# A fused attention and MLP kernel: quads 0 and 1 scored in three rounds of 512 columns with a shared 64-row key tile, and a new order of the first table

## Chip, cores and metric

The kernel runs on one core of a Trainium2 chip. The metric is the device time of one execution in microseconds. Engines: PE is TensorE (matmuls), PEld its weight loads, DVE is VectorE, ACT is ScalarE, POOL is GpSimd, SP is SyncE. POOL issues most of the loads of the first part, and ACT does the exponentials and gelus.

## What is computed

The reference is a causal attention with a forget gate, then an MLP with a tanh gelu. Cut to what matters:

```python
# q, k, v: (8, 8, 576, 64), f: (8, 8, 576); w_in: (512, 2048), w_out: (2048, 512)
scores = scale * np.matmul(q, k.transpose(0, 1, 3, 2))
cum = np.cumsum(np.log(np.clip(f, 0.0001, 1.0)), axis=-1)
scores = np.where(causal, -1e9, scores + cum[:, :, :, None] - cum[:, :, None, :])
attn = softmax(scores)
x = np.matmul(attn, v).transpose(0, 2, 1, 3).reshape(4608, 512)
h = x @ w_in
out = gelu_tanh(h) @ w_out
```

## The kernel before, in words

**Quads.** The 64 heads are taken four at a time; quad i holds heads 4(i % 2) to 4(i % 2) + 3 of batch i // 2. Two quads fill one batch's rows of xT, the input of the MLP. The MLP goes in nine chunks of 512 rows of x; chunk 0 needs all of quads 0 and 1 except the last 64 queries.

**Scores.** The scores are computed with keys on the partitions and queries along the columns, so the key tile is the stationary operand. kT has 64 zero columns ahead of the keys and 64 behind. Causality removes all queries ahead of a key tile, so only pieces (key tile, column in pt, first query, number of queries) are computed. For quads from 2 on, `pieces` (L51) packs them in 1536 columns: the tiles "low" (64 zero rows, then keys 0 to 63) and "high" (keys 512 to 575, then 64 zero rows) share the columns 0 to 63, since each has zeros where the other has keys. The 1536 columns are done in three rounds of 512. For quads 0 and 1, `split_pieces` (L61) holds them in four rounds of 384, 512, 320 and 384 columns, 1600 in all; "high" has columns of its own there, and no "low" is used. Queries 0 to 255 (part 0) and 256 to 575 (part 1) are finished separately, so that the first half of chunk 0 can begin early.

**One round** (`scores`, L267): two passes c over the two halves of the head dimension (32 rows each), one matmul for each piece and head into PSUM (two heads in a tile of two banks, pool psS of two tiles, which the J tiles use too), then an exponential by ACT into pt for each pair of heads (L293). Word S does four heads side by side, word H one pair g of heads. After that come the causal masks: word M by affine select on POOL (L299), word m by a product on DVE (L329).

**Products** (`product`, L333): the denominators (word D: stationary w_bf, then two transposes and a reciprocal on DVE, L374 to L378) and the two halves of the head dimension (word V: stationary vw, then a product on DVE into xT, L387). With a part they use one bank of pool psM (two banks, L341), without one psO or psS (L355). vw is v times the weight of its key (word vw on DVE, VW on POOL, L233). Where "low" is used, word CL or cl copies the first 64 rows of vw to the low tile (L238), and w_bf needs the same copy (`cast_w`, L777; word w on ACT for quads 0 and 1, W on DVE for the others).

**The order.** The kernel has no loop order of its own: all engines follow tables of words (L71 to L111), written out by hand, each issuing its instructions in the order of the words. Inside an engine the order is strict; across engines semaphores order. FRONT covers quads 0 to 6 and chunks 0 and 1; SECOND, STEADY, FLUSH and LAST the rest. The words of FRONT that matter here:

- `B.n.w`: n idle matmuls of w columns (L258); `BK.i.n`: n idle matmuls of 512 columns that read kT of quad i and so wait for its transpose (L264).
- `SC`, `CT`, `CE.n`: running sum of log f on DVE, its transposes on PE (L749), the weights by exponentials on ACT (L754), n = 1 those of quads 2 on.
- `TK.i`, `TQ.i`: transposes of k and q on DVE (L216). `LK.i`, `LQ.i`: their loads (L209).
- `LP.t`: v tile t of batch 0 (tile 4 has only 64 rows); `LC.b.t` of batch b; `WI.c`: quarter c // 2 of w_in's columns, half c % 2 of its rows (L198); `WO.c`: quarter c of w_out's rows (L202). All are issued by POOL, in the order of the words, among its masks. A load waits until the eighth load before it has landed.
- `J.half.g`, `j.half.g.n`: 256 rows of chunk 0 times quarter g of w_in, 16 units of one matmul each (L439); a quarter needs WI.2g for its rows 0 to 255 and WI.2g+1 for the others. j has its PSUM tile in psO (one buffer) and goes n units on; J uses psS. `RJ` copies a finished tile out of psO, `GJ` is the gelu of a j tile, J has its own.
- `F.c.n`, `f.c.n`: n units of the second matmul of chunk c; f in tiles of 32 columns, the form of D and V. In chunk 0 a unit is one matmul of 512 columns, in the order of w_out's quarters, eight units for each in the first pair of row blocks (L692).
- `I`, `U`, `G`, `UW`, `PW`, `X`: the first matmul of chunk 1 and the sums for the Strassen products, and a preload of the exponential table.

PE changes its tile form between words: 128 x 128 for B, BK, J and F, 32 x 128 for S and H, 128 x 32 for D, V and f.

Of the kernel before, what the change touches and what calls it, by code (L numbers as in the profile page):

```python
# [16 lines left out]
def kernel(  # L17
# [53 lines left out]
    FRONT = """  # L71
        B.1.128 B.1.512 B.1.256 SC B.8.512 B.1.256 B.1.512 B.1.128 LP.0 LP.1 CT B.2.512 WI.1 B.1.256 TK.0 B.1.128 B.1.128 BK.0.2 WI.0 LP.4
        BK.0.1 B.1.512 CE.0 TQ.0 B.1.512 CE.1 LP.3 B.1.512 BK.0.1 S.0.0 B.1.128 B.1.128 LP.2 TK.1 M.0.0 w.0 WI.5 BK.0.1 B.3.512 WI.2 H.0.2.1
        WI.3 B.1.128 TQ.1 BK.0.1 B.1.128 B.1.128 B.1.256 B.1.128 BK.1.1 B.1.512 H.0.1.0 WI.4 D.0.0 vw.0.0 vw.1.0 H.0.2.0 B.2.512 BK.1.1
        B.1.128 H.1.0.1 H.1.0.0 M.1.0 B.1.128 B.1.512 B.1.128 B.1.512 B.1.128 V.0.1.0 H.1.2.0 H.0.1.1 V.0.0.0 H.0.3.0 D.1.0 V.1.1.0 j.0.0.4
        M.0.1 UT LQ.2 WI.7 V.1.0.0 H.0.3.1 H.1.3.1 j.0.0.4 j.0.0.8 H.1.1.0 vw.0.1 WI.6 H.1.1.1 RJ.0.0 M.0.3 D.0.1 LK.2 WO.1 WO.0 j.0.1.8
        VW.1.1 H.1.2.1 tr H.1.3.0 M.1.3 V.0.1.1 V.0.0.1 J.0.2 j.0.1.8 M.1.1 D.1.1 V.1.0.1 V.1.1.1 GJ.0.1 W.1 TQ.2 J.0.3 J.1.1 GJ.0.0 J.1.3
        J.1.0 U.0 WO.2 J.1.2 LK.3 WO.3 LQ.3 LC.1.0 PW.2.1 PW.2.2 F.0.3 LC.1.3 f.0.2 LC.1.4 LC.1.1 LC.1.2 TK.2 f.0.1 LK.4 LQ.4 f.0.1 S.2.0
        F.0.5 TK.3 m.2.0 F.0.5 S.2.2 F.0.2 f.0.5 TQ.3 f.0.2 S.2.1 f.0.3 LV.2.1 F.0.6 S.3.0 F.0.2 m.2.1 vw.2 cl.2 F.0.2 f.0.1 LV.2.0 X M.2.2
        D.2 M.3.0 LQ.5 f.0.1 S.3.1 VW.3 f.0.2 V.2.0 LK.5 TQ.4 TK.4 f.0.4 S.3.2 LV.3.1 LQ.6 f.0.1 m.3.1 f.0.3 LK.6 V.2.1 M.3.2 f.0.3 S.4.1  # L80
        f.0.1 F.0.5 VW.4 TQ.5 F.0.1 X H.4.2.0 H.4.2.1 D.3 f.0.1 cl.3 H.4.0.0 H.4.0.1 V.3.1 v.3.0 vw.5 U.1 f.0.2 m.4.2.2 I.1.2 I.1.1 UW.2.4
        TK.6 I.1.0 CL.5 U.2 m.4.2.3 I.1.3 I.1.5 TQ.6 U.3 TK.5 I.1.4 G.0 I.1.6 M.4.1 I.1.7 F.1.1 G.1.1.2 cl.4 F.1.5 LV.3.0 F.1.5 S.5.0 F.1.5
        M.5.0 F.1.7 m.4.0 F.1.2 UW.2.3 F.1.2 LK.8 F.1.7 LK.7 D.4 S.5.1 F.1.17 LQ.8 F.1.1 S.5.2 M.5.2.3 M.5.2.2 f.1.2 V.4.0 f.1.1 M.5.1 f.1.8
        LQ.7@m.3.1 f.1.1 V.4.1 S.6.0 M.6.0 f.1.4 D.5 f.1.10 S.6.1 f.1.1 M.6.1 f.1.2 V.5.1 vw.6 F.1.4 CL.6 F.1.5 S.6.2 m.6.2.3 V.5.0 f.1.4
        m.6.2.2 f.1.3
    """
# [174 lines left out]
    def keep_busy_after(i, n):  # L261

        for _ in range(n):
            nc.tensor.matmul(idle_ps[0][:, 0:512], idle[:, 0:128], kT[i % 2][:, 64:64 + 256, :].rearrange("p s c -> p (s c)"),  # L264
                             start=True, stop=True)

    def scores(i, r, groups=((0, 1, 2, 3),)):  # L267

        qq, p = qT[i % 2], pt[i % 2]
        if i < 2:  # L270
            off, n = split_rounds[r]
            todo = [(key, col - off, q0, nq) for (key, col, q0, nq) in split_pieces[r]]
        else:
            off, n = rounds[r]
            todo = []
            for (key, col, q0, nq) in pieces:
                a, z = max(col, off), min(col + nq, off + n)
                if a < z:
                    todo.append((key, a - off, q0 + a - col, z - a))
        for heads in groups:  # L280
            tiles = {g: psS.tile([128, 2, 512], FP32, name="ps_s", tag="s") for g in sorted({h // 2 for h in heads})}
            for c in range(2):
                for j, (key, c0, q0, nq) in enumerate(todo):
                    for h in heads:
                        nc.tensor.matmul(  # L285
                            tiles[h // 2][:, h % 2, c0:c0 + nq],
                            key_columns(i, key, h, c),
                            qq[32 * h:32 * h + 32, q0:q0 + nq, c],
                            start=(c == 0 and j == 0), stop=(c == 1),
                            skip_group_check=True,  # L290
                        )
            for g, t in tiles.items():
                nc.scalar.activation(p[:, 2 * g:2 * g + 2, off:off + n], t[:, :, 0:n], AF.Exp, scale=scale)  # L293

    def mask(i, r, keys=None):
        p = pt[i % 2]

# [4 lines left out]

        if i < 2:
            for (key, col, n) in diagonals(r, keys):
                keep(p[:, :, col:col + n], [[0, 4], [1, n]])
            return
# [11 lines left out]

    def mask_by_product(i, r, keys=None):
        p = pt[i % 2]  # L320
        if i < 2:
            todo = [(0, col, n) for (key, col, n) in diagonals(r, keys)]
        else:
            todo = [(1 if key == "low" else 0, col, 128) for (key, col, q0, nq) in pieces
                    if (not keys or key in keys) and q0 == 128 * (0 if key == "low" else 9 if key == "high" else key)
                    and rounds[r][0] <= col < rounds[r][0] + 512 and key != 0]
# [4 lines left out]
        return did

    def product(i, groups, spare, part=None):  # L333
        p = pt[i % 2]
        if part is not None:
            s0, s1 = parts[part]
            po = psM.tile([128, 512], FP32, name="po_m", tag="m")
            for (key, col, q0, nq) in sorted(sum(split_pieces[1:] if part else split_pieces[:1], []), key=lambda x: HIGH if x[0] == "high" else x[0]):
                for (r0, lhsT, h) in groups:
                    w = lhsT(HIGH if key == "high" else key)  # L340
                    nc.tensor.matmul(  # L341
                        po[r0:r0 + w.shape[-1], q0 - s0:q0 - s0 + nq], w, p[:, h, col:col + nq],
                        start=(key == 0), stop=(key == (HIGH if part else 1)),
                        skip_group_check=True,
                    )
# [431 lines left out]
    def cast_w(copy, n):  # L777
        i0, i1 = (0, 2) if n == 0 else (2, NQ)
        copy(w_bf[:, i0:i1, 0:NT, :], wT[:, i0:i1])
        if n:  # L780
            copy(w_bf[64:128, :, LOW, :], wT[0:64, :, 0, :])
# [114 lines left out]
```

## Time and profile before

| what | value |
|---|---|
| median of 3 runs | 321.03 us (321.01 to 321.31) |
| the profiled execution, in all | 321.58 us |
| its span, first to last instruction | 319.9 us |
| busy PE / DVE / ACT / POOL | 314.1 / 243.3 / 213.0 / 108.2 us |
| HBM read / written | 36.85 / 9.44 MB |
| PE clock granted | 1.00 |

A line of the timeline has start, duration, engine, line, operation, written and read tiles, tile form, shape and count; adjacent instructions of one line are merged. A line of the busy times by stretches has the stretch, its length, busy time of each engine with the number of instructions, the granted clock, the mean busy share of the 16 DMA engines (over 1 where transfers overlap) and GB/s. A line of the DMA issues has destination and source, queue, count, size and microseconds from issue to landing. Line numbers are those of the kernel before.

### The profile page before, as it was taken

The numbers are of one execution on the slowest core, as the hardware profiler recorded it, in microseconds if no ns is written. First come the engines' busy times: TensorE is split into PE (matmuls) and PEld (weight loads), VectorE is DVE, ScalarE is ACT, GpSimd is POOL, SyncE is SP. The second block draws the span as 40 slices with busy tenths as digits, with TensorE's granted clock in tenths as the row PEclk, the third lists the DMA queues.
The fourth block names the chain that finished last, engine by engine and source line by source line (L and its number), as shares of the span: only waits on it lengthen the run. The fifth ranks groups of instructions, "written<-read, shape, count | busy, mean of one in ns | idle before, by whom it ended". The sixth has DMA issues, their size and how long they took to land.

```text
span 319.9 us, 11741 instructions
## 1 busy us (share of the span) xinstructions
PE 314.1 (98%) x5292; PEld 220.7 (69%) x5311; DVE 243.3 (76%) x368; ACT 213.0 (67%) x248; POOL 108.2 (34%) x146
## 2 busy tenths in 40 slices
PE   8999999999999999999999999999999999999996
PEld 3467834445776567776778877767776786688785
DVE  7675638698978879879877998599886866597674
ACT  3676777866766776878667867787596744836610
POOL 8789625600340416400851065305610150000000
PEclk9999999999999999999999999999999999999999
DMA  7999998951273911594129411971002111010213
GB/s 125 229 199 196 207 234 202 220 150 37 54 130 103 200 22 37 115 209 77 37 75 223 104 39 30 209 160 38 5 33 68 35 33 38 24 43 2 98 35 99
DMA packets 47491, 33.41 MB, mean 104 GB/s; under 512 B 29777, under 2 KB 42193, under 8 KB 47441
## 3 DMA queue, kind: packets, MB, share of 16 engines
q0 software_dynamic: 9632, 15.99, 28.3%
q1 hardware_dynamic: 37664, 16.60, 19.4%
q8 instruction: 41, 0.67, 0.9%
q10 hardware_dynamic: 144, 0.07, 0.1%
q14 instruction: 10, 0.07, 0.1%
HBM read 36.85 MB, written 9.44 MB: 145 GB/s over the span
## 4 chain that ended last, share of the span: by engine, by line
PE 98%; DVE 1%; issue 1%
PE ps_w L619 31%; PE ps_h L403 19%; PE ps_s L285 10%; PE ps_q L539 10%; PE po L355 9%; PE ps_h L439 5%; PE pso L692 4%; PE ps_u L487 4%; PE idle_ps L258 3%; PE po_m L341 2%; PE ps_p L619 1%; PE ps_o L355 0%; PE idle_ps L264 0%; DVE xT L387 0%; PE cum_ps L749 0%
## 5 line engine op out<-in xcount | busy, mean ns | idle before, releaser
L293 ACT ACTIVATE pt<-ps_s 128x1024 bf16<-128x1024 f32 (+2 forms) x100 | 94.0, 991 | 37.5 <-PE ps_s L285 35.9
L299 POOL TENSOR_SCALAR_AFFINE_SELECT pt<-pt 128x512 bf16<-128x512 bf16 (+3 forms) x70 | 43.3, 629 | 108.3 <-ACT pt L293 85.6
L403 PE MATMUL ps_h<-xT,w_in_sb 128*128 128x512 bf16 (+1 forms) x307 | 65.5, 357 | 0.8 <-issue 0.2
L403 PEld LDWEIGHTS <-w_in_sb 128*128 128x128 bf16 x320 | 31.1, 98 | 26.5 <-issue 0.6
L411 ACT ACTIVATE gT<-ps_h 128x1024 bf16<-128x1024 f32 x34 | 34.6, 1018 | 20.3 <-PE ps_h L403 20.1
L619 PEld LDWEIGHTS <-gT 128*32 128x32 bf16 (+1 forms) x1177 | 43.9, 97 | 5.7 <-issue 2.2
L619 PE MATMUL ps_w<-w_out_sb,gT 128*32 128x256 bf16 (+1 forms) x996 | 42.7, 273 | 0.0
L619 PEld LDWEIGHTS <-gsum 128*32 128x32 bf16 (+1 forms) x909 | 35.1, 97 | 3.9 <-issue 1.7
L285 PE MATMUL ps_s<-qT,kT 32*128 32x64 bf16 (+5 forms) x896 | 35.2, 261 | 0.0
L555 DVE TENSOR_TENSOR usnap<-ps_q,usnap 128x1024 f32<-128x1024 f32 x15 | 17.9, 1221 | 17.3 <-PE ps_q L539 12.7
L619 PE MATMUL ps_w<-usum,gsum 128*32 128x256 bf16 (+1 forms) x752 | 29.8, 273 | 0.0
L233 POOL TENSOR_TENSOR vw<-v_nat,wT 128x1280 bf16<-128x1280 f32 (+1 forms) x12 | 27.4, 2279 | 2.7 <-DMA v_nat<-in_v_dram 2.4
L285 PEld LDWEIGHTS <-kT 32*128 32x128 bf16 x896 | 16.2, 92 | 16.8 <-issue 10.2
L636 DVE COPY snap<-ps_w 128x512 f32<-128x512 f32 x32 | 21.8, 682 | 6.5 <-PE ps_w L619 6.3
L550 ACT ACTIVATE gT<-usnap 128x1024 bf16<-128x1024 f32 x15 | 15.8, 1052 | 11.0 <-DVE usnap L555 10.7
L387 DVE TENSOR_TENSOR xT<-po,rb 128x576 bf16<-128x576 f32 x26 | 19.5, 751 | 4.6 <-PE po L355 4.4
L355 PE MATMUL po<-pt,vw 128*32 128x64 bf16 (+4 forms) x624 | 22.6, 278 | 0.0
L355 PEld LDWEIGHTS <-vw 128*32 128x32 bf16 x672 | 14.6, 97 | 9.6 <-issue 3.0
L216 DVE STREAM_TRANSPOSE kT<-k_c 128x576 f32<-128x576 f32 x16 | 19.4, 1244 | 2.1 <-DMA k_c<-in_k_dram 2.1
L216 DVE STREAM_TRANSPOSE qT<-q_c 128x576 f32<-128x576 f32 x16 | 19.8, 1245 | 0.3 <-DMA q_c<-in_q_dram 0.3
L209 POOL DMA_DIRECT2D k_c<-in_k_dram x16 | 9.1, 572 | 29.0 <-DVE kT L216 17.4
L539 PEld LDWEIGHTS <-w_in_sb 128*128 128x128 bf16 x160 | 15.6, 98 | 2.1
(135 smaller groups left out, 489.6 us busy)
## 6 DMA issues: line engine op xcount, KB each, us to landing
out_dram<-o_st SPq DMA_DIRECT2D x35, 256.0 KB, 2.2
k_c<-in_k_dram POOLq DMA_DIRECT2D x16, 288.0 KB, 5.5
q_c<-in_q_dram POOLq DMA_DIRECT2D x16, 288.0 KB, 6.6
v_nat<-in_v_dram SPq DMA_DIRECT2D x16, 256.0 KB, 5.3
v_nat<-in_v_dram SPq DMA_DIRECT2D x20, 128.0 KB, 5.3
v_nat<-in_v_dram POOLq DMA_DIRECT2D x8, 256.0 KB, 10.0
w_in_sb<-in_moe_w_in_dram POOLq DMA_DIRECT2D x8, 256.0 KB, 8.6
w_out_sb<-in_moe_w_out_dram POOLq DMA_DIRECT2D x4, 512.0 KB, 10.6
```

The costliest lines, as they stand in the source:

```text
L216: return nc.vector.transpose(out=dst.rearrange("p s c -> p (s c)").bitcast(FP32) .rearrange("p (t a) -> p a t", a=n), in_=src.rearrange("p ...
L233: return eng.tensor_mul(vw[i % 2][:, t0:t1], vb[:, t0:t1, h0:h0 + 4, :], wT[:, i, t0:t1, :].unsqueeze(3).to_broadcast([128, t1 - t0, 4, D]))
L285: nc.tensor.matmul(tiles[h // 2][:, h % 2, c0:c0 + nq], key_columns(i, key, h, c), qq[32 * h:32 * h + 32, q0:q0 + nq, c], start=(c == 0 an ...
L293: nc.scalar.activation(p[:, 2 * g:2 * g + 2, off:off + n], t[:, :, 0:n], AF.Exp, scale=scale)
L299: nc.gpsimd.affine_select(out=x, in_=x, compare_op=ALU.is_ge, fill=0.0, base=0, pattern=pattern, channel_multiplier=-1)
L355: nc.tensor.matmul(po[r0:r0 + w.shape[-1], 448 + q0:448 + q0 + nq], w, p[:, h, col:col + nq], start=(key in (0, "low")), stop=(key in ("lo ...
L387: nc.vector.tensor_mul(xT[:, 2 * u + x, r0 + s0:r0 + s1], po, rbs[i, part])
L403: nc.tensor.matmul(ph[:, j, n * cols:(n + 1) * cols], w_in_sb[:, dt, 128 * ft:128 * ft + 128], xT[:, dt, h0:h0 + cols], start=(dt == 0 and ...
L411: nc.scalar.activation(gelus(c, 2 * pr, 2), ph, AF.Gelu_apprx_tanh)
L539: nc.tensor.matmul(ps[:, k, HC * n:HC * n + HC], w[:, d, 128 * n:128 * n + 128], x[:, d, :], start=(first and n == 0 and d == 0), stop=(d ...
L619: nc.tensor.matmul(ps[c0:c0 + width, n, cols[0]:cols[1]], x[:, j, 128 * n + c0:128 * n + c0 + width], w[:, j, cols[0]:cols[1]], start=(fir ...
L636: copy(kept[name], ps)
```

## The change

Quads 0 and 1 get their own list of pieces in the packed 1536 columns, with "low" and "high" on the columns 0 to 63, and the three rounds of the other quads. A piece that would cross the border of the two parts (query 256) or of a round is cut there, so there are nine pieces instead of seven. Round 0 holds all of part 0 and the high tile. `scores`, `mask` and `mask_by_product` use one path for all quads, `product` picks the pieces of its part by their first query, and `cast_w` now copies the low rows in both of its calls, where the copy in W covered all quads before. CL.0 and CL.1 come in; the words of round 3 (H.0.3.x, H.1.3.x, M.x.3) go.

```diff
-    split_rounds = [(1152, 384), (0, 512), (512, 320), (832, 384)]
-    split_pieces = [
-        [(0, 1152, 0, 256), (1, 1408, 128, 128)],
-        [(0, 0, 256, 320), (3, 320, 384, 192)],
-        [(1, 512, 256, 320)],
-        [(2, 832, 256, 320), ("high", 1152, 512, 64)],
+    early_pieces = [
+        ("low", 0, 0, 64),
+        (0, 64, 64, 192),
+        (1, 256, 128, 128),
+        (1, 384, 256, 128),
+        (0, 512, 256, 320),
+        (3, 832, 384, 192),
+        (1, 1024, 384, 192),
+        (2, 1216, 256, 320),
+        ("high", 0, 512, 64),
     ]
...
+    def layout(i):
+        return early_pieces if i < 2 else pieces
...
         qq, p = qT[i % 2], pt[i % 2]
-        if i < 2:
-            off, n = split_rounds[r]
-            todo = [(key, col - off, q0, nq) for (key, col, q0, nq) in split_pieces[r]]
-        else:
-            off, n = rounds[r]
-            todo = []
-            for (key, col, q0, nq) in pieces:
+        off, n = rounds[r]
+        todo = []
+        for (key, col, q0, nq) in layout(i):
...
-            for (key, col, q0, nq) in sorted(sum(split_pieces[1:] if part else split_pieces[:1], []), key=lambda x: HIGH if x[0] == "high" else x[0]):
+            mine = [x for x in early_pieces if s0 <= x[2] < s1]
+            for (key, col, q0, nq) in sorted(mine, key=lambda x: {"low": -1, "high": HIGH}.get(x[0], x[0])):
                 for (r0, lhsT, h) in groups:
-                    w = lhsT(HIGH if key == "high" else key)
+                    w = lhsT({"low": LOW, "high": HIGH}.get(key, key))
...
         copy(w_bf[:, i0:i1, 0:NT, :], wT[:, i0:i1])
-        if n:
-            copy(w_bf[64:128, :, LOW, :], wT[0:64, :, 0, :])
+        copy(w_bf[64:128, i0:i1, LOW, :], wT[0:64, i0:i1, 0, :])
```

FRONT is new as a whole; SECOND, STEADY and the others keep their words. Up to the end of J, FRONT before reads (L72 to L78):

```
B.1.128 B.1.512 B.1.256 SC B.8.512 B.1.256 B.1.512 B.1.128 LP.0 LP.1 CT B.2.512 WI.1 B.1.256 TK.0 B.1.128 B.1.128 BK.0.2 WI.0 LP.4
BK.0.1 B.1.512 CE.0 TQ.0 B.1.512 CE.1 LP.3 B.1.512 BK.0.1 S.0.0 B.1.128 B.1.128 LP.2 TK.1 M.0.0 w.0 WI.5 BK.0.1 B.3.512 WI.2 H.0.2.1
WI.3 B.1.128 TQ.1 BK.0.1 B.1.128 B.1.128 B.1.256 B.1.128 BK.1.1 B.1.512 H.0.1.0 WI.4 D.0.0 vw.0.0 vw.1.0 H.0.2.0 B.2.512 BK.1.1
B.1.128 H.1.0.1 H.1.0.0 M.1.0 B.1.128 B.1.512 B.1.128 B.1.512 B.1.128 V.0.1.0 H.1.2.0 H.0.1.1 V.0.0.0 H.0.3.0 D.1.0 V.1.1.0 j.0.0.4
M.0.1 UT LQ.2 WI.7 V.1.0.0 H.0.3.1 H.1.3.1 j.0.0.4 j.0.0.8 H.1.1.0 vw.0.1 WI.6 H.1.1.1 RJ.0.0 M.0.3 D.0.1 LK.2 WO.1 WO.0 j.0.1.8
VW.1.1 H.1.2.1 tr H.1.3.0 M.1.3 V.0.1.1 V.0.0.1 J.0.2 j.0.1.8 M.1.1 D.1.1 V.1.0.1 V.1.1.1 GJ.0.1 W.1 TQ.2 J.0.3 J.1.1 GJ.0.0 J.1.3
J.1.0 U.0 WO.2 J.1.2 LK.3 WO.3 LQ.3 LC.1.0 PW.2.1 PW.2.2 F.0.3
```

and after the change:

```
SC LP.0 B.1.128 B.1.512 LP.3 B.8.512 B.1.512 B.1.128 B.2.512 TK.0 B.1.256 B.1.128 B.1.128 BK.0.2 LP.1 B.1.512 TQ.0 S.0.0 BK.0.1
B.1.512 B.1.128 CT CE.1 H.0.1.0 TK.1 CE.0 WI.1 w.0 B.1.128 BK.0.1 B.3.512 B.1.128 TQ.1 LP.2 WI.3 B.1.128 B.1.256 vw.0.0 WI.0 M.0.0
WI.2 LQ.2 H.1.0.0 H.1.0.1 M.1.0 LP.4 B.1.128 B.1.128 BK.0.1 BK.1.1 BK.0.1 CL.0 H.0.2.0 D.0.0 WI.4 V.0.0.0 WI.5 WI.6 WI.7 H.0.1.1
V.0.1.0 M.0.1 BK.0.1 B.1.128 B.1.128 B.1.512 B.1.128 B.1.256 vw.1.0 CL.1 H.0.2.1 H.1.2.1 UT B.1.512 LK.2 D.1.0 V.1.0.0 B.1.512
V.1.1.0 H.1.2.0 M.0.2 j.0.0.4 j.0.0.4 j.0.0.8 M.1.2 VW.1.1 H.1.1.0 H.1.1.1 WO.0 M.1.1 RJ.0.0 LC.1.1 LK.3 D.0.1 LQ.3 j.0.1.8 j.0.1.8
J.0.2 vw.0.1 GJ.0.1 V.0.0.1 TQ.2 GJ.0.0 tr PW.2.1 D.1.1 J.0.3 V.1.0.1 V.0.1.1 V.1.1.1 J.1.2 J.1.1 J.1.0 J.1.3 F.0.3 W.1 WO.1 WO.2
WO.3 LC.1.3 LC.1.2 F.0.2
```

Behind J both tables hold the same numbers of F and f units (64 for chunk 0, 97 for chunk 1), the same S, D, V and I words in a slightly different order, and a few masks, copies and sums on another engine (m.3.2 for M.3.2, M.4.2.3 for m.4.2.3, CL.3 for cl.3, cl.5 for CL.5, PW.2.4 for UW.2.4).

More of the change, by code (lines that the diff above doesn't have):

```diff
@@ L76 @@
[L76 to L79, printed above, removed]
@@ L98 @@
+        Q.0.2 Q.0.2 LB.2.3 TK.3 LB.2.4 LK.5 i.0.3.4 Q.0.2 TK.4 TQ.4 F.-1.99 I.0.6 i.0.7 G.0 S.3.0 X G.1.1.2 f.0.16 M.3.0 D.2 VW.3 f.0.12
+        S.3.1 M.3.1 V.2.0 f.0.13 S.3.2 M.3.2 CL.3 V.2.1 VW.4 f.0.15 S.4.0 D.3 f.0.10 V.3.0 M.4.0 CL.4 S.4.1 f.0.14 M.4.1 V.3.1 S.4.2 F.0.12
+        M.4.2
     """
@@ L301, in keep @@
                 fill=0.0, base=0, pattern=pattern, channel_multiplier=-1)
[L303 to L306, printed above, removed]
         if r == 0:
@@ L309, in mask @@
             keep(p[64:128, :, 0:128].rearrange("p h (b x) -> p h b x", x=64), [[0, 4], [0, 2], [1, 64]])
-        for (key, col, q0, nq) in pieces:
-            if key in (keys or (1, 2, 3)) and rounds[r][0] <= col < rounds[r][0] + 512:
+        for (key, col, q0, nq) in layout(i):
+            if key in (keys or (1, 2, 3)) and q0 == 128 * key and rounds[r][0] <= col < rounds[r][0] + 512:
                 keep(p[:, :, col:col + 128], [[0, 4], [1, 128]])
-    def diagonals(r, keys):
-        return [(4 if key == "high" else key, col, min(nq, 128)) for (key, col, q0, nq) in split_pieces[r]
-                if q0 == (512 if key == "high" else 128 * key) and (not keys or (4 if key == "high" else key) in keys)]
     def mask_by_product(i, r, keys=None):
         p = pt[i % 2]
[L321 to L326, printed above, removed]
+        todo = [(1 if key == "low" else 0, col, 128) for (key, col, q0, nq) in layout(i)
+                if (not keys or key in keys) and q0 == 128 * (0 if key == "low" else 9 if key == "high" else key)
+                and rounds[r][0] <= col < rounds[r][0] + 512 and key != 0]
         did = None
@@ L337, in product @@
             po = psM.tile([128, 512], FP32, name="po_m", tag="m")
-            for (key, col, q0, nq) in sorted(sum(split_pieces[1:] if part else split_pieces[:1], []), key=lambda x: HIGH if x[0] == "high" else x[0]):
+            mine = [x for x in early_pieces if s0 <= x[2] < s1]
+            for (key, col, q0, nq) in sorted(mine, key=lambda x: {"low": -1, "high": HIGH}.get(x[0], x[0])):
                 for (r0, lhsT, h) in groups:
-                    w = lhsT(HIGH if key == "high" else key)
+                    w = lhsT({"low": LOW, "high": HIGH}.get(key, key))
                     nc.tensor.matmul(
                         po[r0:r0 + w.shape[-1], q0 - s0:q0 - s0 + nq], w, p[:, h, col:col + nq],
-                        start=(key == 0), stop=(key == (HIGH if part else 1)),
+                        start=(key in (0, "low")), stop=(key == ("high" if part else 1)),
                         skip_group_check=True,
```

34 lines of the change are left out of this document (15 added, 19 removed).

## The prediction

> **What bounds the kernel now.** First the page: its engine line and the head of the chain that ended last.
>
> ```profile
> span 319.9 us, 11741 instructions
> PE 314.1 (98%) x5292; PEld 220.7 (69%) x5311; DVE 243.3 (76%) x368; ACT 213.0 (67%) x248; POOL 108.2 (34%) x146
> PE 98%; DVE 1%; issue 1%
> ```
>
> TensorE is the bound, and it works through its instructions in program order. So the time is the sum of what stands on PE: real matmuls, idle matmuls (words B and BK), and waits. The change touches quads 0 and 1 and the order of FRONT, so I read next where idle matmuls lie: busy time of L258 (B) by stretches, then L264 (BK).
>
> ```profile
> 6.30:18.20 11.90, 5.37 (x27) 2.12 (x27) 1.00 1.10 213
> 18.20:39.00 20.80, 0.00 (x0) 0.00 (x0) 1.00 1.20 200
> ...
> 6.30:18.20 11.90, 2.33 (x7) 0.74 (x8) 1.00 1.10 213
> ```
>
> All fill lies ahead of 18.20 us; behind it PE has real work only. The timeline of PE shows the marks that I use:
>
> ```profile
> 8.31 0.81 PE L258 MATMUL idle_ps<-idle 128*128 128x512 bf16 x3
> 8.96 0.38 PE L264 MATMUL idle_ps<-kT,idle 128*128 128x512 bf16 x1
> 9.27 0.52 PE L285 MATMUL ps_s<-qT,kT 32*128 32x256 bf16 x16
> ...
> 18.20 0.61 PE L439 MATMUL ps_h<-xT,w_in_sb 128*128 128x256 bf16 x4
> ...
> 22.78 1.05 PE L439 MATMUL ps_h<-xT,w_in_sb 128*128 128x256 bf16 x8
> ...
> 25.49 2.79 PE L439 MATMUL ps_h<-xT,w_in_sb 128*128 128x256 bf16 x24
> ...
> 28.22 0.70 PE L341 MATMUL po_m<-pt,w_bf 128*32 128x320 bf16 x20
> 28.75 1.50 PE L341 MATMUL po_m<-pt,vw 128*32 128x320 bf16 x40
> 30.18 8.91 PE L439 MATMUL ps_h<-xT,w_in_sb 128*128 128x256 bf16 x80
> 38.92 1.79 PE L692 MATMUL pso<-w_out_sb,gT 128*128 128x512 bf16 x18
> ```
>
> Three idle matmuls of 512 columns start 8.31 to 8.96: 0.217 us each, 0.42 ns a column. From the fourth (8.96) to S.0.0 (9.27) it is 0.31, so a change of tile form costs 0.1. A J unit costs (38.92 - 30.18) / 80 = 0.109. Chunk 0's first half-matrix (the 128 J units) begins at 18.20 and ends at **38.92**; from there on everything is dense, and both tables hold the same units. So I ask when J ends after the change.
>
> The second resource in that stretch is the DMA queue. The DMA share by stretches of 4 us (fifth column from PE on, before GB/s):
>
> ```profile
> 12.00:16.00 4.00, 3.95 (x54) 1.83 (x53) 2.66 (x6) 2.80 (x5) 3.47 (x6) 1.00 1.17 220
> 20.00:24.00 4.00, 3.99 (x62) 2.64 (x62) 3.34 (x6) 3.10 (x4) 3.99 (x8) 1.00 1.20 199
> 24.00:28.00 4.00, 4.00 (x75) 3.27 (x69) 1.20 (x3) 3.65 (x7) 3.59 (x5) 1.00 1.13 184
> ```
>
> The share is over 1 throughout: the loads wait for each other. POOL's timeline gives their issue (LP.0 and LP.1; LQ.2; WI.7 and WI.6), the DMA view of single issues the time to landing, in the same order:
>
> ```profile
> 4.25 1.81 POOL L186 DMA_DIRECT2D v_nat<-in_v_dram  x2
> 19.60 0.57 POOL L209 DMA_DIRECT2D q_c<-in_q_dram  x1 [0.21 <-DVE rb L378]
> 20.17 1.41 POOL L198 DMA_DIRECT2D w_in_sb<-in_moe_w_in_dram  x2
> ```
>
> ```profile
> v_nat<-in_v_dram POOLq DMA_DIRECT2D x1, 256.0 KB, 8.0
> v_nat<-in_v_dram POOLq DMA_DIRECT2D x1, 256.0 KB, 7.8
> q_c<-in_q_dram POOLq DMA_DIRECT2D x1, 288.0 KB, 6.6
> w_in_sb<-in_moe_w_in_dram POOLq DMA_DIRECT2D x1, 256.0 KB, 7.4
> w_in_sb<-in_moe_w_in_dram POOLq DMA_DIRECT2D x1, 256.0 KB, 7.9
> ```
>
> LP.0 lands at 12.25, LP.1 (issued 5.15) at 12.95, LQ.2 at 26.2, WI.7 at 27.57, WI.6 (issued 20.87) at **28.77**: in issue order, a piece of w_in every 1.2 to 1.4 us. J.0.3 needs both of the last; it starts at 30.18, so before has 1.4 us of slack at this gate.
>
> **The change part by part.** *PE work.* In columns: B and BK fall from 18,688 to 16,768: 1,920 x 0.42 ns = -0.81 us. The scores keep 1,600 columns for each quad and each of the two passes over c (the shared tile is still two matmuls of 64), but S.0.0, where four heads run side by side, now covers 576 columns instead of 384, and a pair of heads the rest: -384 columns, -0.16. Three fewer changes of tile form up to J's end, -0.3; one more behind it, +0.1. Sum **-1.17**, if nothing waits.
>
> The products get 9 matmuls a head instead of 7, the scores 9 pieces instead of 7: 80 matmuls more. A group of 1,600 columns on 24 matmuls, two of them sets of 64, in the chain by time:
>
> ```profile
> 50.98 0.68 PE po L355 x24
> ```
>
> 1,600 x 0.42 = 0.67: short pieces cost nothing over their columns, and I take 0. "TensorE: Matmul & The Clock Gate" of the Trainium skill (section "Wait — 56ns, not 53.3ns?") speaks against this: start to start never falls below about 25 ns however few the columns, by which 80 more matmuls would add up to 2.0 us; this row disagrees, since four tiles run side by side.
>
> *ACT.* Its groups from 9 to 27 us, by shape:
>
> ```profile
> L293 ACT ACTIVATE pt<-ps_s 128x768 bf16<-128x768 f32 x8 | 6.2, 809 | 2.9 <-PE ps_s L285 2.8
> L293 ACT ACTIVATE pt<-ps_s 128x1024 bf16<-128x1024 f32 x4 | 4.0, 1021 | 1.6 <-PE ps_s L285 1.6
> L293 ACT ACTIVATE pt<-ps_s 128x640 bf16<-128x640 f32 x4 | 2.8, 706 | 0.6 <-PE ps_s L285 0.6
> ```
>
> 16 exponentials of 13.0 us become 12 of 1.02 = 12.3: -0.7 on an engine that idles 5 us here. I give it nothing; without ACT's idle it would be worth those 0.7.
>
> *Added on the side.* Two copies CL on DVE, and in w.0 a second copy on ACT. DVE's CL of later quads, and the copy of the low rows inside W.1:
>
> ```profile
> L238 DVE COPY vw<-vw 64x256 bf16<-64x256 bf16 x11 | 2.4, 221 | 0.3
> ```
>
> ```profile
> 31.77 1.09 DVE L781 CAST w_bf<-wT 64x64 bf16<-64x64 f32 x1
> ```
>
> CL costs 0.22 each. The second copy of w.0 (an eighth of L781's columns, on ACT) lies between 0 and 1.09; I take 0.25, nearer to CL. Masks stay five a quad on POOL.
>
> *The chain up to the first J.* DVE's timeline:
>
> ```profile
> 7.24 1.22 DVE L216 STREAM_TRANSPOSE qT<-q_c 128x576 f32<-128x576 f32 x1
> 11.13 1.26 DVE L216 STREAM_TRANSPOSE qT<-q_c 128x576 f32<-128x576 f32 x1 [0.28 <-DMA q_c<-in_q_dram]
> 14.33 1.25 DVE L233 TENSOR_TENSOR vw<-v_nat,wT 128x512 bf16<-128x512 f32 x2
> 21.34 1.22 DVE L419 COPY usum<-ps_h 128x1024 f32<-128x1024 f32 x1 [0.26 <-PE ps_h L439]
> ```
>
> S.0.0 may start when TQ.0 ends, 8.5 instead of 9.27, since CT and its fill move behind it. That lead is lost again: H.1.0.0 waits for TQ.1 at 12.4 as before, and V.0.0.0 for vw.0.0 and CL.0 on v tiles 0 and 1, of which LP.1 now stands behind LP.3. LP.1 lands one load later than its 12.95: 0.7 (its own distance from LP.0) to 1.3 (that of the w_in pieces). With 14.2, half of L233's 1.25 and CL's 0.22 it is 15.05. Behind V.0.0.0 on PE stands H.0.1.1, behind that its exponential and five more steps with fill. Ten half rounds with an exponential each, from 9.2 on at 1.02, and half a microsecond of idle ACT put the first J at about 20.
>
> *The loads.* Up to WI.7 the queue carries the same eighteen loads in both tables, and it never runs dry. So the last piece lands at 28.8 again; it is WI.7 now, behind WI.6, WI.5 and WI.4. WI.5 lands two pieces sooner, 28.8 - 2 x 1.3 = **26.2**. WI.0, eighth before, is eleventh: behind it come WI.2, LQ.2, the half tile LP.4 and the four last, 5 x 1.3 + 1.4 + 0.6, so it lands at about 20.3.
>
> *J behind the loads.* j.0.0 starts at 20.4 (WI.0; the chain above agrees). Its 16 units 1.75, two half rounds 0.8, D.0.1 0.6, j.0.1 1.75 (RJ's 1.22 copy is done by 23.5): 25.3. J.0.2 runs two units and waits for WI.5. On PE behind it stands all the rest: from 26.2, 14 units 1.53, V.0.0.1 and D.1.1 of 0.53 each and a change of form 1.2, so J.0.3 starts at 29.0 and WI.7 has landed. J.0.3 1.75, three V (one 0.53 and a pair 1.43 by the rows at 28.22 and 28.75) 1.96 and 0.1, 64 units 7.0: J ends at **39.85**, +0.93. From the gate of WI.7 alone, 28.8 + 10.8 = 39.6, it is +0.7. With the change of form behind it +0.8 to +1.03; the landing of WI.5 is interpolated, so I take the middle, +0.95.
>
> *Behind J.* LC.1.1, LK.3 and LQ.3 now stand ahead of WO.1. POOL's issue of w_out's first two pieces and their landing:
>
> ```profile
> 23.11 1.51 POOL L202 DMA_DIRECT2D w_out_sb<-in_moe_w_out_dram  x2
> ```
>
> ```profile
> w_out_sb<-in_moe_w_out_dram POOLq DMA_DIRECT2D x1, 512.0 KB, 9.6
> w_out_sb<-in_moe_w_out_dram POOLq DMA_DIRECT2D x1, 512.0 KB, 11.5
> ```
>
> A piece takes 35.3 - 32.7 = 2.6. WO.1 then lands at 28.8 + two pieces 5.2 + k, k, q and v of 1.3 to 1.5 = 39.6, and is needed at the ninth F unit, 39.85 + 8 x 0.217 = 41.6: covered by 2.0, and nothing to pay. Had J ended at 37.7, this cover would be gone.
>
> The sum goes against span 319.9 (this execution took 321.58 in all, the median of the runs is 321.03): span 320.85, time **322.0**.
>
> **The rivals.** *A, nothing waits.* The loads land 2 us sooner than I derive, and PE goes through its 1.17 us less: 319.9, faster. For it: fill and forms are counted, not estimated. Against it: then J.0.3 would start near 27, 1.8 us ahead of the last landing, with a share above 1. It decides where WI.5 lands before 24.2. "DMA: Bandwidth & Descriptors" of the Trainium skill (section "Anatomy of one DMA — SWDGE (gpsimd) path") would have it so: 2.0 us and 436 KB a microsecond put each load's moving at 0.6 us; the landings 1.2 us apart here disagree.
>
> *B, the chain ahead of J is late.* LP.1, behind LP.3, lands after 15.1: V.0.0.0 waits, and H.0.1.1 and all behind it slip. Up to 0.9 us (25.3 to 26.2) the wait for WI.5 swallows it; beyond, each tenth is a tenth: 322.7 for a slip of 1.6. w.0's copy at its upper end, 0.8 more on ACT, would use up that cover alone. Against it: LP.1 has 2.1 us from 12.95 to there, and one load lies between.
>
> *C, the gates are looser.* If pieces land 0.6 to 1.2 us sooner than interpolated (before's landings spread by that much between v tiles), J ends between 38.7 and 39.3: 320.8 to 321.5, no difference.
>
> **How the numbers follow.** The measurement tells about 0.2%, 0.64 us, from no change. Forecast 0.50 (321.5 to 322.5, a tenth of it within 0.64), A 0.16, B 0.12, C 0.22. Faster 0.16, same 0.27, slower 0.57. The range leaves out A and the far end of B: 320.7 to 323.0.
>
> **What would show it.** In the profile after: S.0.0 at about 8.5; first J unit at 20 to 20.5 instead of 18.20; a gap on PE inside J.0.2 that ends with WI.5's landing near 26.2; J.0.3 at about 29; first F unit at 39.6 to 39.9. If the first F unit starts before 38.9, the gates were wrong; if J.0.2 starts after 26.3, the chain ahead of it was (B). A wait for w_out behind J would be one that I cost at nothing.

## The result and the profile after

The changed kernel takes **321.77 us** (median of 12 executions, 321.55 to 322.99); the kernel before, run beside it, 321.05 (320.94 to 322.0). The ratio is 1.0025, with a 95% interval of 1.0017 to 1.0033: 0.7 us slower, at the bound of what can be told from no change. The profiled execution took 321.8 us, its span is 320.0.

The head of the page after: span, busy time by engine, and the chain that ended last, by engine.

```profile
span 320.0 us, 11903 instructions
PE 312.3 (98%) x5375; PEld 221.8 (69%) x5395; DVE 243.8 (76%) x370; ACT 212.3 (66%) x245; POOL 110.7 (35%) x146
...
PE 90%; DVE 4%; ACT 2%; issue 1%; DMA 1%; DVEq 0%
```

PE is busy 1.8 us less than before, so the work did shrink. But the chain, 98% PE before, now has a tenth outside PE. About half of that tenth lies in its first 25 us, most of the rest between 60 and 100 us. Chain of waits of the kernel after, in order of time (start, duration, what):

```profile
0.81 2.87 DMA f_all<-in_f_dram
...
7.40 1.23 DVE qT L221
...
9.44 1.92 ACT pt L297 x2
11.36 0.51 ACT wT L747 x2
11.87 0.91 ACT pt L297
12.78 0.34 ACT wT L747 x2
13.14 0.22 ACT w_bf L772
13.37 0.20 ACT w_bf L773
...
16.91 0.66 PE idle_ps L263 x5
...
18.58 0.32 PE idle_ps L263
...
19.23 0.46 DVE den L367
```

Read it from the top: S.0.0 waits for the transpose of q (qT), and then five microseconds are ACT's alone. Three exponentials and a fourth of 1.03 behind L773 stand there, and between them stand the weights of CE.1 and CE.0 (L747) and both copies of w.0 (L772, L773). H.0.2.0 on PE begins when the fourth exponential ends. Behind that stand idle matmuls that still cost their time.

The marks on PE, timeline of the kernel after: S.0.0, the first J tile (j.0.0), j.0.1 with J.0.2, J.0.3, the first F units.

```profile
8.68 0.70 PE L289 MATMUL ps_s<-qT,kT 32*128 32x64 bf16 x40 [0.41 <-DVE qT L221]
...
20.58 1.92 PE L432 MATMUL ps_h<-xT,w_in_sb 128*128 128x256 bf16 x16
...
23.82 3.80 PE L432 MATMUL ps_h<-xT,w_in_sb 128*128 128x256 bf16 x32
...
28.71 1.92 PE L432 MATMUL ps_h<-xT,w_in_sb 128*128 128x256 bf16 x16
...
39.50 1.89 PE L685 MATMUL pso<-w_out_sb,gT 128*128 128x512 bf16 x7
```

Where the 0.7 us came from needs a second look at the kernel before, which is the first experiment.

### The profile page after: what moved, and what is told of

Same layout as the page of the kernel before. It is cut to its first block, busy times and chain, and to the rows that moved or that the text cites. A ratio compares the mean times of both kernels' runs of the same rounds, so it can differ in the third digit from the quotient of the medians.

```text
span 320.0 us, 11903 instructions
## 1 busy us (share of the span) xinstructions
PE 312.3 (98%) x5375; PEld 221.8 (69%) x5395; DVE 243.8 (76%) x370; ACT 212.3 (66%) x245; POOL 110.7 (35%) x146
## 4 chain that ended last, share of the span: by engine, by line
PE 90%; DVE 4%; ACT 2%; issue 1%; DMA 1%; DVEq 0%
PE ps_w L612 29%; PE ps_h L396 19%; PE ps_q L532 10%; PE po L348 9%; PE ps_s L289 8%; PE ps_h L432 5%; PE pso L685 4%; PE ps_u L480 4%; PE po_m L334 1%; ACT pt L297 1%; DVE xT L380 1%; DMA f_all<-in_f_dram 1%; DVE den L367 1%; PE ps_p L612 1%; DVE f_all L721 0%
## 5 line engine op out<-in xcount | busy, mean ns | idle before, releaser
L297 ACT ACTIVATE pt<-ps_s 128x1024 bf16<-128x1024 f32 x96 | 93.2, 1020 | 40.5 <-PE ps_s L289 38.8
L303 POOL TENSOR_SCALAR_AFFINE_SELECT pt<-pt 128x512 bf16<-128x512 bf16 (+2 forms) x69 | 44.6, 653 | 93.0 <-ACT pt L297 66.6
L289 PE MATMUL ps_s<-qT,kT 32*128 32x64 bf16 (+4 forms) x928 | 34.9, 257 | 0.8 <-DVE qT L221 0.4
L289 PEld LDWEIGHTS <-kT 32*128 32x128 bf16 x928 | 17.2, 92 | 16.3 <-issue 9.7
```

Source lines behind the costliest of these rows:

```text
L289: nc.tensor.matmul(tiles[h // 2][:, h % 2, c0:c0 + nq], key_columns(i, key, h, c), qq[32 * h:32 * h + 32, q0:q0 + nq, c], start=(c == 0 an ...
L303: nc.gpsimd.affine_select(out=x, in_=x, compare_op=ALU.is_ge, fill=0.0, base=0, pattern=pattern, channel_multiplier=-1)
```

## The experiments

**1. The kernel before, once more.** No edit. The profiled execution of before that the prediction used took 321.58, half a microsecond over its median.

> The kernel before, unchanged. The trace of before has J end at 38.92, the first I unit at 65.12 and a span of 319.9, and its execution lies 0.5 us above the median of its runs. Theory 1: that half microsecond was lost behind J in that one execution; then J ends at 38.9 again, the first I unit comes at about 64.6 and the span is 319.3. Theory 2: it was lost ahead of J; then J ends at about 38.4. Theory 3: the trace is typical and the same marks come back within 0.1.

Median 321.11 beside 321.08, ratio 1.000 [0.9991, 1.0009], span 319.4. None of the three theories holds as a whole: of the half microsecond 0.2 lay ahead of S.0.0 (9.27 there, 9.06 here), the rest behind the first I. PE's timeline: S.0.0, the first J units, the first F units behind J, the first I unit; then the first I unit of the kernel after.

```profile
9.06 0.52 PE L285 MATMUL ps_s<-qT,kT 32*128 32x256 bf16 x16
...
17.98 0.61 PE L439 MATMUL ps_h<-xT,w_in_sb 128*128 128x256 bf16 x4
...
38.70 1.79 PE L692 MATMUL pso<-w_out_sb,gT 128*128 128x512 bf16 x18
...
64.90 1.31 PE L403 MATMUL ps_h<-xT,w_in_sb 128*128 128x512 bf16 x4
```

```profile
65.24 1.03 PE L396 MATMUL ps_h<-xT,w_in_sb 128*128 128x512 bf16 x4 [0.16 <-DVE xT L380]
```

Against this execution the change loses 0.80 us up to the end of J (38.70 to 39.50), and wins back 0.46 from there to the first I (26.20 to 25.74). From the first I to about 100 us it takes 34.88 instead of 34.72, and the spans differ by 0.6. So the loss lies ahead of 39.5 us, and all others but experiment 9 look there. S.0.0 itself begins 0.38 sooner (8.68); from S.0.0 to J's end it takes 30.82 us instead of 29.64.

Three things could set J's end after the change: the chain of the exponentials, the idle matmuls behind it, and the loads of w_in. Experiments 2, 3 and 5 change one of them each, experiment 4 two.

**2. Without the idle matmuls behind V.0.1.0.** The fill of the chain's lower half goes.

```diff
-V.0.1.0 M.0.1 BK.0.1 B.1.128 B.1.128 B.1.512 B.1.128 B.1.256 vw.1.0 CL.1 H.0.2.1 H.1.2.1 UT B.1.512 LK.2 D.1.0 V.1.0.0 B.1.512
+V.0.1.0 M.0.1 vw.1.0 CL.1 H.0.2.1 H.1.2.1 UT LK.2 D.1.0 V.1.0.0
```

> The kernel after without the three groups of fill between V.0.1.0 and H.1.2.0 (eight idle matmuls, 2,688 columns). Theory chain: these stand on the path that sets the first J, so J starts at about 19.9 instead of 20.58 and J's end moves from 39.50 to about 38.8: -0.7 us. Theory gates: J.0.2 and J.0.3 then wait for WI.5 (25.8) and WI.7 (28.65), and J ends no sooner than 39.25: at most -0.25. Theory masks: D.0.1 waits for M.0.2 behind the loads on POOL, J's end moves by -0.2.

Median 322.55 (321.25 to 324.32), ratio 1.0043 [1.0023, 1.0063]: no gain, but a loss, which no theory had. Busy times by stretches of this run (the column after POOL is the granted clock of PE), and j.0.0 on PE's timeline:

```profile
17.00:20.00 3.00, 2.36 (x58) 1.20 (x54) 2.70 (x8) 2.36 (x3) 3.00 (x5) 1.00 1.20 211
20.00:24.00 4.00, 4.00 (x34) 2.54 (x32) 1.11 (x3) 1.02 (x1) 3.91 (x8) 0.58 1.07 164
```

```profile
20.06 3.53 PE L432 MATMUL ps_h<-xT,w_in_sb 128*128 128x256 bf16 x16
```

The first J came half a microsecond sooner (0.69 counted from S.0.0), as the fill's absence would have it. Then the granted clock fell to 0.58 for 4 us, and the 16 units took 3.53 instead of 1.92. Where the fill stood, the longest gap on PE is 0.44 us (start less the end of the columns before, at 0.42 ns each). The clock is lost in some executions only: six of the eleven, with a mean clock of 0.999 to 1.0, took 321.25 to 322.55, the five others, at 0.989 to 0.994, 322.86 to 324.32. So this fill does a job: it holds the clock.

**3. A new order of loads.** LP.4 and WI.4 ahead of the mask M.1.0, LQ.2 behind WI.7; nothing on PE changes.

```diff
-WI.2 LQ.2 H.1.0.0 H.1.0.1 M.1.0 LP.4 ... V.0.0.0 WI.5 WI.6 WI.7 H.0.1.1
+WI.2 LP.4 WI.4 H.1.0.0 H.1.0.1 M.1.0 ... V.0.0.0 WI.5 WI.6 WI.7 LQ.2 H.0.1.1
```

> The kernel after with the last loads of w_in sooner on POOL: LP.4 and WI.4 ahead of M.1.0, LQ.2 behind WI.7. WI.5 should land near 24.0 and WI.7 near 26.4 instead of 25.8 and 28.65. Theory gates: J.0.2 and J.0.3 were held by them, time -0.5 or more. Theory chain: PE does not wait for them, J ends at 39.5 within 0.2 and the time stays.

Median 321.60 (321.35 to 322.21), ratio 1.0018 [1.001, 1.0027], inside the interval of the kernel after. V.0.0.0 and j.0.0 of this run:

```profile
15.94 0.35 PE L334 MATMUL po_m<-pt,vw 128*32 128x64 bf16 x12 [0.57 <-DVE vw L243]
...
20.96 1.92 PE L432 MATMUL ps_h<-xT,w_in_sb 128*128 128x256 bf16 x16
```

Now LP.1 was the latest: V.0.0.0 waited for vw, begun at 14.68 instead of 14.55, and for its low copy, which took 0.48 instead of 0.22; the first J came at 20.96. J.0.2 no longer waits (its 32 units with j.0.1 take 3.65), and still nothing is gained: the loads alone are not what binds.

**4. Experiments 2 and 3 together.**

> e1 and e2 together. Theory chain with gates close beneath it: J ends at about 38.55, -0.95 us, more than e1 and e2 together. Theory chain alone: as e1. Theory gates alone: as e2.

Median 321.23 (320.73 to 323.69), ratio 1.0019 [1.0001, 1.0036]; the mean clock was 0.994 or 0.995 in three of twelve executions, which took 322.66 to 323.69. The nine others, at 0.999 or 1.0, have a median of 321.07, 0.7 less than the kernel after; the six of experiment 2 that kept the clock have 321.6, as has experiment 3. So fill and loads together are worth 0.7 where the clock holds, and each alone less than 0.2.

**5. CT, CE.0 and CE.1 ahead of S.0.0.** That takes the weights out from between the exponentials.

```diff
-... B.2.512 TK.0 ... BK.0.2 LP.1 B.1.512 TQ.0 S.0.0 BK.0.1 B.1.512 B.1.128 CT CE.1 H.0.1.0 TK.1 CE.0 WI.1 w.0
+... B.2.512 CT TK.0 ... BK.0.2 CE.0 CE.1 LP.1 B.1.512 TQ.0 S.0.0 BK.0.1 B.1.512 B.1.128 H.0.1.0 TK.1 WI.1 w.0
```

> The kernel after with CT, CE.0 and CE.1 ahead of S.0.0, as before. In after the four CE exponentials (0.85 us net) stand between the exponentials of the scores on ACT, which runs without a gap from 9.42 to 17.53. Theory ACT chain: H.1.0.0's exponential starts at 12.9 instead of 13.59 and J's end moves by up to -0.6. Theory LP.1: V.0.0.0 waits for vw.0.0 on LP.1 (14.55) at the same moment, so J's end moves by no more than -0.15. Theory of two walls: as LP.1 here, and only e6 gains.

Median 321.83 (321.41 to 322.56), ratio 1.0020 [1.0011, 1.0029]: no gain. Its profiled execution took 322.56. PE's timeline: S.0.0, j.0.0, then j.0.1 with two units of J.0.2, and the rest of J.0.2.

```profile
9.62 0.70 PE L289 MATMUL ps_s<-qT,kT 32*128 32x64 bf16 x40 [1.21 <-DVE qT L221]
...
20.84 1.92 PE L432 MATMUL ps_h<-xT,w_in_sb 128*128 128x256 bf16 x16
...
24.09 2.14 PE L432 MATMUL ps_h<-xT,w_in_sb 128*128 128x256 bf16 x18
26.64 1.70 PE L432 MATMUL ps_h<-xT,w_in_sb 128*128 128x256 bf16 x14 [0.40 <-DMA w_in_sb<-in_moe_w_in_dram]
```

Two things are to be seen. From S.0.0 to the first J it takes 11.22 instead of 11.90, so the chain did get shorter. But q's first load landed late in this execution, S.0.0 began at 9.62, and nothing ahead of it covers that. And here stands the gap that the prediction had drawn: two units of J.0.2, then a wait for WI.5 of half a microsecond (18 units end at about 26.1). This run's chain of waits leads back from that wait to ACT: an exponential that ends at 15.92, the mask M.1.0 behind it until 17.83, the issue of WI.5 at 19.20 and its landing at 26.59.

**6. LP.1 ahead of LP.3 again,** as in the kernel before.

```diff
-SC LP.0 B.1.128 B.1.512 LP.3 ... BK.0.2 LP.1 B.1.512 TQ.0 S.0.0
+SC LP.0 B.1.128 B.1.512 LP.1 ... BK.0.2 LP.3 B.1.512 TQ.0 S.0.0
```

> The kernel after with LP.1 ahead of LP.3, as before. vw.0.0 starts at about 13.3 instead of 14.55. Theory LP.1: V.0.0.0 and what stands behind it come sooner, J's end moves by -0.5 or more. Theory ACT chain: H.0.2.0 waits for ACT until 14.67 as before, D.0.0 and V.0.0.0 stand behind it, J's end moves by no more than -0.15. Theory of two walls: as ACT chain here.

Median 321.63 (321.39 to 322.8), ratio 1.0020 [1.0011, 1.0029], inside the interval of the kernel after. vw.0.0 on DVE, and H.0.2.0 on PE:

```profile
13.53 0.69 DVE L238 TENSOR_TENSOR vw<-v_nat,wT 128x512 bf16<-128x512 f32 x1 [1.21 <-DMA v_nat<-in_v_dram]
```

```profile
14.84 0.63 PE L289 MATMUL ps_s<-qT,kT 32*128 32x192 bf16 x8 [0.28 <-ACT pt L297]
```

vw.0.0 began a microsecond sooner (13.53 instead of 14.55), and nothing followed it: PE waited for the exponential, and j.0.0 began at 20.59 as after the change (S.0.0 0.17 later). LP.1 is not on the path there.

**7. Experiments 3, 5 and 6 together,** with all fill kept.

> e4, e5 and e2's order of the loads together, with all fill kept. Theory of two walls (ACT chain and LP.1 side by side, the w_in gates close beneath): J starts at about 19.8 and ends at 38.6, time 320.9 or less, with the granted clock at 1.00. If one of the walls alone held, it is as the better of e4 and e5.

Median 321.23 (320.77 to 321.57) beside 321.07, ratio 1.0003 [0.9994, 1.0012]: the loss is gone. j.0.0 and the first F units on PE:

```profile
20.36 1.92 PE L432 MATMUL ps_h<-xT,w_in_sb 128*128 128x256 bf16 x16
...
39.13 1.24 PE L685 MATMUL pso<-w_out_sb,gT 128*128 128x512 bf16 x5
```

Though S.0.0 began at 9.12 here (q late again), J ends 0.37 sooner than after the change. The three edits that gave nothing each give half a microsecond together: the limits lie within a few tenths of each other. Counted from S.0.0, J ends after 30.82 us in the kernel after, 31.25 in experiment 3, 30.60 in 5, 30.70 in 6 and 30.01 here. Which of the three edits are needed is not settled: experiment 5 alone already brings S.0.0 to the first J down to 11.22 (11.24 here), and what this run adds is that J.0.2 no longer waits; CE early with the new loads, but LP.1 late, was not run.

**8. The layout alone.** The new code with FRONT of before: words of round 3 dropped, CL.0 and CL.1 behind vw.0.0 and vw.1.0, nothing else moved.

> The layout of after with the table of before (words of round 3 dropped, CL.0 and CL.1 behind vw.0.0 and vw.1.0). Theory order: the loss comes from the new order ahead of J; the layout alone saves 384 columns and some changes of form on PE and 0.7 us on ACT, J ends at about 38.2 and the time is 320.6. Theory layout: S.0.0 with 576 columns, CL and w.0's copy delay D.0.0 and the first J whatever the order; J ends at 39 or later and the time is 321.5 or more.

Median 325.75 (325.54 to 326.48, 4 executions), ratio 1.0148 [1.0134, 1.0162]. The matmuls of D.0.0 and D.1.0 that waited for a mask, on PE:

```profile
13.88 0.23 PE L335 MATMUL po_m<-pt,w_bf 128*1 128x128 bf16 x4 [0.33 <-POOL pt L304]
...
20.06 0.23 PE L335 MATMUL po_m<-pt,w_bf 128*1 128x128 bf16 x4 [0.41 <-POOL pt L304]
```

In round 0 three masks now stand ahead of the denominators instead of two, and PE waits for them. In this execution (the slowest of the four, with a clock of 0.57 from 20 to 24 us) J ends at 41.69, and 2 us more are lost in chunk 1, where PE waits 1.8 us at 95 us for something that the profile doesn't name: 3.0 and 2.0 us of its 5.0 over before's span. The clock is not the main part, since the three others, at 1.0, took 325.54 to 325.79. The two waits for masks are 0.7 of the 3.0; the rest was not taken apart. With the old order the layout loses 4.7 us: the way of the theory of the layout, and far beyond its bound of 321.5.

**9. The order behind J alone.** The kernel before up to J's end, and behind it the words of after, without those that the old head has done.

```diff
-J.1.2 LK.3 WO.3 LQ.3 LC.1.0 PW.2.1 PW.2.2 F.0.3 LC.1.3 f.0.2 LC.1.4 ...
+J.1.2 LK.3 WO.3 LQ.3 PW.2.1 LC.1.1 F.0.3 LC.1.3 LC.1.2 F.0.2 LQ.4 TK.2 LC.1.0 F.0.3 S.2.0 ...
```

> The kernel before up to the end of J (its layout, its order), and behind J the order of the kernel after, with the words that the old head has already done left out. Theory: behind J the new order is worth about 0.4 us by itself (J's end to the first I took 25.74 us after the change in two kernels and 26.20 in two profiles of before), and what the change lost lies ahead of J; then the span from J's end to the first I is 25.7 to 25.8 here, J ends at 38.7 to 38.9, and the time is 320.6 to 320.7, ratio 0.9987. Rival (the forecast's step): the new order behind J costs one change of form more, +0.1, and the 0.46 belongs to the later end of J (work that other engines have done by then); then J to I takes 26.2 to 26.3 and the time is 321.1 to 321.2, ratio 1.000.

Median 321.05 beside 321.19, ratio 0.9994 [0.9985, 1.0003]: no difference. J ends at 38.70, as before. The scores of H.4.0.0 and H.4.0.1 and the first I here; the same scores of the kernel after; then both marks of the kernel of experiment 10, in which J ends at 38.25:

```profile
60.83 1.46 PE L284 MATMUL ps_s<-qT,kT 32*128 32x64 bf16 x24
...
64.70 1.03 PE L402 MATMUL ps_h<-xT,w_in_sb 128*128 128x512 bf16 x4
```

```profile
61.63 1.14 PE L289 MATMUL ps_s<-qT,kT 32*128 32x64 bf16 x24
```

```profile
60.39 1.14 PE L289 MATMUL ps_s<-qT,kT 32*128 32x64 bf16 x24
...
63.99 2.32 PE L396 MATMUL ps_h<-xT,w_in_sb 128*128 128x512 bf16 x10
```

From J's end to the first I it is 26.00, between the two theories: 0.20 of the 0.46 come from the order, and 0.26 don't. The group of scores near 61 us is 0.32 longer here than after the change, since H.4.0.1 waits until the exponential of H.4.2.0 ends (61.54). The rival's reason for the 0.26, a later J that meets work that others have done by then, does not hold: with J's end at 38.25 the group takes 1.14 and the way to the first I 25.74, and all ten profiled kernels with the new head of FRONT have 25.74 or 25.75, with J's end anywhere from 38.25 to 40.58. So the 0.26 come with the new head, its layout or its order; why ACT begins that exponential later behind its scores with the old head (1.04 us after they begin, 0.73 after the change) stays open.

**10 to 12. Half of the fill removed,** from the kernel of experiment 7 (10, and once more as 12) and from the kernel after (11).

```diff
-H.1.2.1 UT B.1.512 LK.2 D.1.0 V.1.0.0 B.1.512
+H.1.2.1 UT LK.2 D.1.0 V.1.0.0
```

> The kernel of the run with CE early, LP.1 early and the new order of loads (321.23), less the two idle matmuls of 512 columns between D.1.0, V.1.0.0 and V.1.1.0 (2 x 0.213 us); the six idle matmuls behind V.0.1.0 stay. Theory: the fill on this stretch is path as long as PE is ahead of nothing, so PE comes to the first J 0.43 sooner if the clock holds: J ends about 38.7, time 320.8, granted clock 1.00. Rival: the clock gate counts these columns too, and the granted clock falls below 0.9 in 20 to 24 us as it did where all of this fill was taken out; then J's first units run at about half speed, J ends at 39.5 to 40.5 and the time is 321.5 to 322.5.

> The kernel after the change, less the two idle matmuls of 512 columns around D.1.0 and V.1.0.0 (2 x 0.213 us); the loads stand as after the change, where WI.7 landed at 28.65 and J.0.3 began at 28.71. Theory (the loads are a second limit right beneath the chain ahead of J): PE comes to J.0.2 and J.0.3 up to 0.43 sooner and waits there for WI.5 and WI.7, the gap in or ahead of J.0.2 or J.0.3 is 0.3 to 0.4, J ends at 39.3 to 39.6, and the time is 321.6 to 321.8. Rival (only the chain ahead of J counts): no gap at J.0.2 and J.0.3, J ends at about 39.1, 321.35. Granted clock 1.00 in both.

> The same kernel as the one with half of the fill removed, CE early, LP.1 early and the new order of loads, which gave 320.76 beside 321.19 of the kernel before, ratio 0.9992 [0.998, 1.0003]. If it is faster than both kernels, its median is again 320.6 to 320.9 and the interval of the ratio, with two slower executions of eleven in it the last time, lies at or below 1.000; if that was the chip, it is 321.0 to 321.3.

From experiment 7's kernel: 320.76 beside 321.19, ratio 0.9992 [0.998, 1.0003], and again 320.72 beside 321.08, ratio 0.9996 [0.9985, 1.0008]. From the kernel after: 321.75 beside 321.08, ratio 1.0023 [1.0014, 1.0032]. The first one's stretches and marks:

```profile
17.00:20.00 3.00, 2.77 (x64) 1.69 (x59) 2.56 (x7) 2.45 (x3) 3.00 (x5) 1.00 1.24 225
20.00:24.00 4.00, 3.90 (x65) 3.03 (x64) 2.64 (x6) 2.60 (x4) 3.92 (x8) 1.00 1.24 203
```

```profile
8.42 0.70 PE L289 MATMUL ps_s<-qT,kT 32*128 32x64 bf16 x40 [0.27 <-DVE qT L221]
...
38.25 1.89 PE L685 MATMUL pso<-w_out_sb,gT 128*128 128x512 bf16 x8
```

The clock held at 1.00, and J ended at 38.25, 1.25 sooner than after the change (0.26 of it since S.0.0 began sooner; against experiment 7's kernel, counted from S.0.0, it is 0.18). The median beats the kernel after by 1.0 us in both, and lies 0.4 below the kernel before; but two or three executions in each took 321.6 to 322.6, and the interval of the ratio reaches over 1. Faster than the kernel before is likely, not shown.

From the kernel after, the same edit gave nothing in the median. Its profiled execution was the fastest of the eleven (321.36), with q early:

```profile
23.47 3.67 PE L432 MATMUL ps_h<-xT,w_in_sb 128*128 128x256 bf16 x32
...
39.02 1.24 PE L685 MATMUL pso<-w_out_sb,gT 128*128 128x512 bf16 x4
```

There is no gap at J.0.2 (32 units in 3.67) or ahead of J.0.3 (28.23), and J ends where the rival had it; the theory's gap is absent. But of the 0.43 that the two idle matmuls took, only 0.22 is won from S.0.0 to the first J (11.68 instead of 11.90): PE now waits 0.39 us there for the transpose of the denominators of D.1.0. The loads had come sooner too: POOL issues the last four behind the mask M.1.0, which waits for an exponential, so they move with the chain. Why the median did not follow stays open: when q landed in the executions without a profile is not known.

## Why the prediction was right or wrong

The number was right, 322.0 against 321.77, and so was the sign, with the difference at the bound of what can be told. But the wait that it rested on was mostly not there: another took its place. That the total came out within 0.3 us is in part luck. J's end moved by 0.58 against the profile that the prediction started from and by 0.80 against experiment 1, not by 0.93, and behind J 0.46 came back up to the first I (0.16 of it was lost again by 100 us) where 0.1 was to be lost.

**PE's own work: right.** PE's busy time fell by 1.8 us against the first profile of before and by 1.4 against experiment 1 (1.17 foretold, with the changes of form). Short pieces are free: a product of the later part (D or V) is 20 matmuls before (0.70 us, the row at 28.22) and 24 after, on PE's timeline:

```profile
27.55 0.71 PE L334 MATMUL po_m<-pt,vw 128*32 128x320 bf16 x24
```

**ACT, "given nothing": the step that failed.** It counted the exponentials (12 of 1.02, right) and took ACT's idle 5 us as a cover. After the change S.0.0 starts sooner, the groups are all 1024 columns, and CE and w.0 come between them: ACT works from 9.42 to 17.53 without a gap, and the path goes through it until 14.62. The chain's duration was nearly right (first J at 20 to 20.4 foretold, 20.58 measured), but by luck: it was summed as ten half rounds with an exponential each, and the path holds four exponentials (3.9 us), then CE.1, CE.0 and w.0 (1.3 us), which were not seen in it, and behind them PE's own work and fill.

**Copies and masks.** CL 0.22 and w.0's second copy 0.20 (0.25 taken). "Masks stay five a quad" is right as a count and missed the point: round 0 has three of them now. POOL's timeline after, M.1.0 and the four last loads behind it:

```profile
15.60 1.85 POOL L303 TENSOR_SCALAR_AFFINE_SELECT pt<-pt 64x256 bf16<-64x256 bf16 x3 [1.09 <-ACT pt L297]
...
18.11 2.85 POOL L203 DMA_DIRECT2D w_in_sb<-in_moe_w_in_dram  x4
```

**S.0.0 at 8.5: right in this execution (8.68), but not firm.** It is the end of TQ.0, which waits for q: 8.42 to 9.62 in the ten profiles of kernels with the new head of FRONT. Before, S.0.0 stood behind fill and CT at 9.06 and 9.27, which hid this.

**The loads: nearly right, for a partly wrong reason.** The first and the last of the four (issued 18.11 and 20.24, in the DMA view of single issues):

```profile
w_in_sb<-in_moe_w_in_dram POOLq DMA_DIRECT2D x1, 256.0 KB, 6.5
w_in_sb<-in_moe_w_in_dram POOLq DMA_DIRECT2D x1, 256.0 KB, 8.4
```

WI.7 lands at 28.65 (28.8 foretold). But "it never runs dry" was not quite so: the share is 1.04 from 20 to 24 us (0.82 from 21 to 22), where it was 1.20 before. What thinned the queue no run isolates.

```profile
20.00:24.00 4.00, 3.97 (x74) 2.83 (x67) 2.54 (x5) 2.02 (x3) 3.91 (x9) 1.00 1.04 176
```

**The wait in J.0.2: wrong in size.** It was to be 0.7 or more (25.5 to 26.2). The 32 units of j.0.1 and J.0.2 take 3.80, against 3.65 without a wait (experiments 2, 3 and 7): 0.15. PE came to it 0.3 later than foretold, WI.5 landed 0.3 sooner; PE's weight loads still show it:

```profile
25.91 1.43 PEld L432 LDWEIGHTS <-w_in_sb 128*128 128x128 bf16 x14 [0.25 <-DMA w_in_sb<-in_moe_w_in_dram]
```

So J's end at 39.50 (39.85 foretold; the terms as listed add up to 39.8) is mostly the chain's doing, with the loads right beneath it. That both limits count, experiments 2 to 7 show: each relieved alone, less than 0.2 in the median; together, half a microsecond or more. Rival B named the chain, but put it down to LP.1; experiment 6 shows that LP.1 was not it in this kernel (with the loads of experiment 3 it was). Rivals A and C needed loads that land 0.6 to 2 us sooner; they did not.

**Behind J, +0.1: wrong.** It was -0.46 up to the first I, of which 0.20 belong to the order behind J and 0.26 to the new head (experiment 9). No wait for w_out came, as foretold.

## What to carry to other kernels

Where an engine idles in the profile before, ask whether it still does once the work ahead of it starts sooner: list everything that stands on that engine between its first and last instruction of the stretch, small words too, and add it up as a chain. If two limits lie within a few tenths of each other, relieving one shows nothing; test them together before calling one harmless. And a load that is issued behind a mask lands when the mask's input lets it, so order it by the engine's waits, not by its place in the table.
